# The projection phase of a gated attention mix: three weight tiles a chunk, measures between evictions, zero matmuls ahead, loads from two queues

## The chip, the core and the metric

The kernel runs on one core of one Trainium2 chip. The metric is the device time of one execution in microseconds. The core has five engines, each with a queue of its own that runs in order: TensorE (PE, matrix products into the eight banks of PSUM), VectorE (DVE), ScalarE (ACT), GpSimd (POOL) and SyncE (SP). SP, ACT and POOL also issue DMAs, which run on sixteen DMA engines. Semaphores order the engines among each other.

## The reference

Two attentions over the same input are mixed by a gate. A has 32 heads with their own keys and values; B has 32 query heads and one shared key and value head. Each head is 18 wide.

```python
x = A_x                                   # 1 x 2048 x 576
g = sigmoid((x * gate_w).sum(-1, keepdims=True))
q, k, v = heads(x @ A_wqkv)               # 32 heads of 18
a = (softmax(q k^T / sqrt(18)) v) @ A_wo
q = heads(x @ B_wq); k = x @ B_wk; v = x @ B_wv      # one k, one v for all heads
b = (softmax(q k^T / sqrt(18)) v) @ B_wo
return g * a + (1 - g) * b
```

## The kernel before

The kernel has two phases. The first projects x; the second, nearly nine tenths of the time, goes through 64 heads. Only the first phase is touched by the change; it is followed by the projection of A's values (`project_v`, L252), which already runs among the first row maxima of the heads, and by the loop over heads.

The transposed input `xT` is 576 x 2048. The left sides of all projections but A's values are laid out as one matrix `wall` of 14 weight tiles of 128 columns (`MT = 14`): B's key, the gate, B's value and B's queries in tiles 0 to 4, A's queries and keys, interleaved by heads, from the end of tile 4 on. The contraction of 576 is split in five blocks of 128 rows (`NKT = 5`); the fifth has 64 rows, which are loaded twice, into both halves of the 128 partitions.

For accuracy each operand is split in a rounded high part and the remainder: `xh`, `xl` of x (L275 on ACT, L276 and L277 on DVE), `wh`, `wl` of a weight tile (L133 on ACT, L134 on DVE). A projection of one weight tile for one chunk of 512 columns of x is 14 matmuls into one PSUM bank (`PROJ`, L210): high by high, low by high, high by low; the second copy of the fifth block holds x's remainder, so that high and low of it are done in one matmul. A bank is then evicted as two 16-bit halves, `ph` by ACT (L214) and `pl` by DVE (L220), scaled by `tv`, a power of two for each row, and the halves are written to DRAM (`qkh` from ACT's queue, `qkl` from POOL's). Tile 0 holds the gate and B's value too: it is copied out unscaled (`pst`, L217), and `shared_v` transposes B's value with four PE transposes (L239).

`tv` balances queries against keys. `measure` takes the largest magnitude of each weight column: DVE reduces over the five blocks (L162), PE transposes the result (L165), DVE reduces again (L166). `balance` reduces these over the columns of each kind (a mask made in DRAM tells which columns are which), has PE transpose and spread the two maxima (L176, L183), and computes the powers of two with some ten short DVE instructions (L185 to L195). It runs twice: for B over tiles 0 to 4, for A over all 14.

The order of the work is written out by hand; each engine runs its part in the order of the program. Loads: SP issues `ones_r`, weight tiles 0 to 4, six x tiles of 256 columns (six buffers `xs`), later x tiles 6 and 7 and weight tiles 5 to 13. A tile is three DMAs (`load5`): four blocks at once and the fifth twice. Then: split weight tile 0, measure tiles 0 to 4, balance, split x tiles 0 and 1 and weight tile 1; for each of four chunks split the next two x tiles, project tiles 0 and 1, and then transpose B's value. `project_rest` splits weight tile 2, measures tiles 5 to 13, balances a second time and projects tiles 2 to 13, splitting the next weight tile a tile ahead. POOL, which does no splits in this phase, issues the loads of B's key and of the first head's queries (`ksb`, `kdb`, `qs`) between chunk 3 and `project_rest`.

PSUM has three banks `ps` for projections and scores, four banks `pm` for transposes and maxima, and `acc`.

Of the kernel before, what the change touches and what calls it, by code (L numbers as in the profile page):

```python
# [21 lines left out]
H = 32  # L22
DH = 18
# [26 lines left out]
def gated_mix_kernel(ctx: ExitStack, tc: tile.TileContext, xT, wall, wv, wo, out):  # L50
# [3 lines left out]
    def dma(o, i, eng=None):  # L54
        o, i = (x.bitcast(F32) if x.dtype == F32R else x for x in (o, i))
        return (eng or nc.sync).dma_start(o, i)  # L56
# [67 lines left out]
        if l is not None:  # L124
            eng_l.tensor_tensor(l, src, h.bitcast(F32), op=OP.subtract)

    def load5(t, src):
        dma(t[:, 0:4, :], src[0:512, :].rearrange("(k p) m -> p k m", p=P))
        dma(t[0:64, 4, :], src[512:576, :])
        dma(t[64:128, 4, :], src[512:576, :])  # L130

    def split_w(st, w, eng_l):
        nc.scalar.activation(w["h"], st, AF.Copy)  # L133
        eng_l.tensor_tensor(w["l"], st, w["h"].bitcast(F32), op=OP.subtract)  # L134

    norm = wpool.tile([P, MT], F32, name="norm", bufs=1)
# [5 lines left out]
    nc.gpsimd.memset(zo[:, 0, :], 0.0)  # L142
    nc.gpsimd.memset(zo[:, 1, :], 1.0)
    nc.gpsimd.memset(tv, 0.0)
    mask_d = dram.tile([4, MT * P], F32, name="mask_d")
    dma(mask_d.rearrange("g (a b) -> (g a) b", b=56), zo[:, 0, :], nc.gpsimd)
    dma(mask_d[0:1, ROW_KB:ROW_KB + DH], zo[0:1, 1, 0:DH], nc.gpsimd)
# [3 lines left out]
            zo[0:H, 1, 0:DH], nc.gpsimd)  # L151
    dma(mask, mask_d.rearrange("g (m p) -> p g m", p=P), nc.gpsimd)

    def load_w(mt):
        st = wpool.tile([P, NKT, P], F32, name="wst", bufs=MT)
        load5(st, wall[mt])
        return st

    def measure(mt, st):

        a = wpool.tile([P, P], F32, name="wabs")
        nc.vector.tensor_reduce(a, st.rearrange("p k f -> p f k"), axis=AX.X, op=OP.max,  # L162
                                apply_absolute_value=True)
# [4 lines left out]
    def balance(g, n):  # L168

        m = wpool.tile([P, 2, MT], F32, name="bm", bufs=1)  # L170
        for i in range(2):
            nc.vector.tensor_tensor(m[:, i, 0:n], norm[:, 0:n], mask[:, g + i, 0:n], op=OP.mult)
        r = wpool.tile([P, 2], F32, name="br", bufs=1)
        nc.vector.tensor_reduce(r, m[:, :, 0:n], axis=AX.X, op=OP.max)
        pt = ps_m.tile([P, 512], F32, name="pm")
        nc.tensor.transpose(pt[0:2, 0:P], r, ident)  # L176
# [12 lines left out]
        nc.vector.tensor_scalar(e[:, 1:2], e[:, 0:1], 1.0, 64.0, op0=OP.mult, op1=OP.add)  # L189
        nc.vector.tensor_scalar(e[:, 0:1], e[:, 0:1], -1.0, 190.0, op0=OP.mult, op1=OP.add)  # L190
        t = wpool.tile([P, 2], F32, name="bt", bufs=1)
        nc.vector.tensor_single_scalar(t.bitcast(I32), e, 23, op=OP.logical_shift_left)
        nc.vector.tensor_scalar(t, t, LIFT, None, op0=OP.mult)
        for i in range(2):
            nc.vector.scalar_tensor_tensor(tv, mask[:, g + i, :], t[:, i:i + 1], tv, op0=OP.mult, op1=OP.add)  # L195

    def prep_w(st):
        w = {y: wpool.tile([P, NKT, P], F32R, name=f"w{y}") for y in "hl"}
        split_w(st, w, nc.vector)
# [5 lines left out]
    def project(mt, c, w):  # L205

        fp = ps_s.tile([P, 512], F32, name="ps")
        cs = slice(c * 512, (c + 1) * 512)
        for n, (a, b, k, kr) in enumerate(PROJ):
            nc.tensor.matmul(fp, w[a][:kr, k, :], X[b][:kr, k, cs], start=(n == 0), stop=(n == len(PROJ) - 1))  # L210
# [3 lines left out]
        nc.scalar.activation(h, fp, AF.Copy, scale=t)  # L214
        if mt == 0 or c == 0 and mt in HAS_K:
            st = stp.tile([P, 512], F32, name="pst", bufs=3)
            nc.scalar.activation(st, fp, AF.Copy)  # L217
            if c == 0:
                KD[mt] = st
        nc.vector.scalar_tensor_tensor(l, fp, t, h, op0=OP.mult, op1=OP.subtract)  # L220
        if c == 1 and mt in HAS_K:
            d = stp.tile([P, 512], F32, name="pd", bufs=1)
            nc.vector.tensor_tensor(d, fp, KD.pop(mt), op=OP.subtract)
            dh, dl = (stp.tile([P, 512], F16, name=f"pd{y}", bufs=1) for y in "hl")
            nc.scalar.activation(dh, d, AF.Copy, scale=t)
            nc.vector.scalar_tensor_tensor(dl, d, t, dh, op0=OP.mult, op1=OP.subtract)
        dma(qk_d[0][mt * P:(mt + 1) * P, cs], h, nc.scalar)
        dma(qk_d[1][mt * P:(mt + 1) * P, cs], l, nc.gpsimd)
        if c == 1 and mt in HAS_K:
            dma(kd_d[0][mt * P:(mt + 1) * P, :], dh, nc.scalar)  # L230
            dma(kd_d[1][mt * P:(mt + 1) * P, :], dl, nc.gpsimd)
        if mt == 0:
            dma(z_d[cs], st[ROW_G:ROW_G + 1, :], nc.scalar)
            return c, st
# [25 lines left out]
            pass  # L260

    WV = []
    with tc.tile_pool(name="xs", bufs=6, side="right") as xsp:
        W = [load_w(mt) for mt in range(5)]
        XS = []

        def load_x(c):
            XS.append(xsp.tile([P, NKT, 256], F32, name="xs"))
            load5(XS[c], xT[:, 256 * c:256 * c + 256])

        def split_x(c):
            xs = XS[c]
            cs = slice(c * 256, (c + 1) * 256)
            xh = X["h"][:, :, cs]
            nc.scalar.activation(xh, xs, AF.Copy)  # L275
# [3 lines left out]
        for c in range(6):  # L279
            load_x(c)  # L280
        WP = [prep_w(W[0])]
        for mt in range(5):
            measure(mt, W[mt])
        balance(0, 5)
        for c in range(2):
            split_x(c)
        WP.append(prep_w(W[1]))
        for c in range(6, 8):
            load_x(c)
        for mt in range(5, MT):  # L290
            W.append(load_w(mt))
# [15 lines left out]
    load_q(0, nc.gpsimd)  # L307

    def project_rest():
        WN = prep_w(W[2])  # L310
        for mt in range(5, MT):
            measure(mt, W[mt])
        balance(2, MT)
# [462 lines left out]
```

## Time and profile before

| | us |
|---|---|
| three runs | 2733.84, 2734.75, 2733.58 (median 2733.84) |
| the profiled execution | 2735.79 |
| its span, from the first instruction to the last | 2734.0 |
| PE busy in the span | 2663.3 |
| first projection matmul (L210) | 23.8 |
| last projection matmul of tiles 0 to 13 begins | 238.3 |
| value projection (L252) | 238.6 to 314.8 |

The profile is of one execution. Its page lists busy times by engine; groups of instructions are given by line, engine, operation and tiles, as `out<-in`, with the shapes, the count, the busy time and mean length in ns, and behind a bar the idle time of the engine just before them with what ended it. PE means matmuls, PEld the loading of weights into TensorE. `SPq` or `ACTq` is the sequencer of the queue that issues a DMA. The chain of waits is followed back from the last instruction, at each step to what released it. Tables by stretch give busy time and count of each engine in that stretch, then the granted TensorE clock, the mean busy share of the sixteen DMA engines and what they moved in GB/s.

### The profile page before, as it was taken

To read this page: it belongs to the slowest core of one execution; us is meant where nothing else is said; L and a number is where in the kernel's file an instruction comes from. 1 tells how busy PE (TensorE), PEld (TensorE's weight loads), DVE (VectorE), ACT (ScalarE), POOL (GpSimd) and SP (SyncE) were. 2 spreads that over 40 slices of the span, in tenths; PEclk is the share of its full clock that TensorE was granted. 3 is DMA by queue.
4 is the path that set the end of the run, shared out by engine and by line. 5 is a ranking of instruction groups with operands and counts; after the bars stand their busy time and mean duration, and the time that the engine had idled before them with its cause. 6 is when DMAs were issued, how large, how long until landed. Compare 5 with 4: busy or idle time off the path is not lost.

```text
span 2734.0 us, 57725 instructions
## 1 busy us (share of the span) xinstructions
PE 2663.3 (97%) x22160; PEld 958.8 (35%) x22160; DVE 2430.7 (89%) x4582; ACT 2384.1 (87%) x4768; POOL 231.0 (8%) x438
## 2 busy tenths in 40 slices
PE   5899999999999999999999999999999999999999
PEld 3688522222222222222222333333333332223444
DVE  5345899999999999999999999999999999998875
ACT  3232499999999999999999999999999999998875
POOL 2221000001000200110110001000100020001000
PEclk9899999999999999999999999999999999999998
DMA  7232100001100100110132112112221122122312
GB/s 197 76 118 90 51 20 20 20 18 53 35 17 23 54 27 20 45 43 20 30 66 85 40 51 84 54 40 57 72 66 47 44 61 64 39 64 88 89 36 94
DMA packets 135321, 151.49 MB, mean 55 GB/s; under 512 B 55709, under 2 KB 104765, under 8 KB 133846
## 3 DMA queue, kind: packets, MB, share of 16 engines
q1 hardware_dynamic: 116156, 123.59, 16.2%
q10 hardware_dynamic: 14120, 13.65, 1.5%
q0 software_dynamic: 4768, 10.56, 1.2%
q8 instruction: 174, 2.85, 0.5%
q14 instruction: 103, 0.84, 0.1%
HBM read 92.02 MB, written 46.45 MB: 51 GB/s over the span
## 4 chain that ended last, share of the span: by engine, by line
ACT 54%; PE 37%; DVE 6%; DMA 2%; SPq 1%; issue 1%; DVEq 0%; ACTq 0%
ACT pt L453 48%; PE acc L459 12%; PE ps L446 11%; ACT xb L412 6%; PE ps L210 6%; PE pm L575 4%; DVE mx L418 3%; PE ps L252 2%; PE pm L409 2%; SPq L56 1%; DVE oe L469 1%; DVE junk L415 1%; DMA xs<-xT 0%; DVE oacc L629 0%; DVE oacc L583 0%
## 5 line engine op out<-in xcount | busy, mean ns | idle before, releaser
L453 ACT ACTIVATE pt<-ps 128x512 f32<-128x512 f32 x4052 | 2093.1, 637 | 68.4 <-PE pm L409 60.2
L418 DVE TENSOR_REDUCE mx<-pm 128x1 f32<-128x512 f32 x3096 | 1940.2, 682 | 89.5 <-PE pm L409 74.6
L446 PE MATMUL ps<-qs,ksb 56*128 56x512 f16 x2688 | 818.4, 380 | 10.8
L409 PE MATMUL pm<-ksb,qs 54*128 54x512 f16 x2364 | 738.5, 383 | 2.6 <-DVE mx L418 1.6
L459 PE MATMUL acc<-pt,vb 128*19 128x512 f32 (+1 forms) x6136 | 592.3, 458 | 1.9
L459 PE MATMUL acc<-pt,vg 128*19 128x256 f32 (+1 forms) x5664 | 579.5, 481 | 2.3 <-DVE oe L469 0.5
L409 PEld LDWEIGHTS <-qs 54*128 54x128 f16 x4096 | 330.0, 93 | 248.1 <-issue 195.2
L446 PE MATMUL ps<-qs,ksa 56*128 56x512 f16 x1364 | 404.4, 379 | 4.8 <-ACT pt L453 1.3
L446 PEld LDWEIGHTS <-ksb 56*128 56x128 f16 x2688 | 175.0, 94 | 622.5 <-issue 573.9
L409 PE MATMUL pm<-ksa,qs 54*128 54x512 f16 x1232 | 384.8, 382 | 0.6 <-ACT xb L412 0.4
L415 DVE CUSTOM_DVE_ANT_0 junk<-pm,xb 128x512 bf16<-128x512 f32 x500 | 339.9, 680 | 0.0
L412 ACT ACTIVATE xb<-pm 128x512 f32<-128x512 f32 x500 | 316.5, 633 | 0.0
L446 PEld LDWEIGHTS <-ksa 56*128 56x128 f16 x1408 | 89.3, 94 | 328.9 <-issue 299.0
L459 PEld LDWEIGHTS acc<-pt,vb 128*19 128x19 f32 x6136 | 104.1, 96 | 223.7 <-issue 206.6
L459 PEld LDWEIGHTS acc<-pt,vg 128*19 128x19 f32 x5664 | 96.0, 97 | 222.9 <-issue 204.9
L428 POOL TENSOR_SCALAR mt<-mt 128x32 f32<-128x32 f32 x64 | 18.6, 290 | 1616.4 <-DVE mt L426 1616.4
L214 ACT ACTIVATE ph<-ps,tv 128x512 f16<-128x512 f32 x56 | 38.5, 687 | 122.0 <-PE ps L210 114.5
L409 PE MATMUL pm<-kdb,qs 54*128 54x512 f16 x372 | 141.5, 380 | 0.0
L220 DVE SCALAR_TENSOR_TENSOR pl<-ps,tv,ph 128x512 f16<-128x512 f32 x56 | 42.0, 751 | 93.8 <-ACT ph L214 75.4
L210 PE MATMUL ps<-xh,wh 128*128 128x512 f32 x280 | 76.4, 403 | 3.3 <-DVE xh L277 2.6
L210 PE MATMUL ps<-xh,wl 128*128 128x512 f32 x280 | 75.1, 399 | 0.0
L469 DVE COPY oe<-acc 128x512 f32<-128x512 f32 x63 | 43.6, 692 | 30.0 <-PE acc L459 29.4
(123 smaller groups left out, 1253.8 us busy)
## 6 DMA issues: line engine op xcount, KB each, us to landing
qs<-qkh SPq DMA_DIRECT2D x244, 72.0 KB
qs<-qkl SPq DMA_DIRECT2D x122, 72.0 KB
onh<-oh SPq DMA_DIRECT2D x32, 256.0 KB
onl<-ol SPq DMA_DIRECT2D x32, 256.0 KB
oih<-onh SPq DMA_DIRECT2D x16, 512.0 KB
oil<-onl SPq DMA_DIRECT2D x16, 512.0 KB
ot<-oe SPq DMA_DIRECT2D x220, 36.0 KB
R<-r_d SPq DMA_DIRECT2D x55, 144.0 KB
```

The source lines that it names most:

```text
L210: nc.tensor.matmul(fp, w[a][:kr, k, :], X[b][:kr, k, cs], start=(n == 0), stop=(n == len(PROJ) - 1))
L220: nc.vector.scalar_tensor_tensor(l, fp, t, h, op0=OP.mult, op1=OP.subtract)
L252: nc.tensor.matmul(fp[:, 0:288], X[b][:kr, k, st_ * P:(st_ + 1) * P], w[a][:kr, k, :], start=(n == 0), stop=(n == len(PROJ) - 1))
L409: nc.tensor.matmul(pm, qs[u % 3][b:b + 54, i * P:(i + 1) * P], k, start=True, stop=True)
L412: nc.scalar.activation(MX["x", u, i], pm, AF.Relu)
L415: nc.vector.tensor_tensor_reduce(junk, pm, MX.pop(("x", u, i)), 1.0, -3e38, op0=OP.add, op1=OP.max, accum_out=MX[u][:, i, c:c + 1])
L418: nc.vector.tensor_reduce(MX[u][:, i, c:c + 1], pm, axis=AX.X, op=OP.max)
L446: nc.tensor.matmul(ps, kst(u)[b:b + 56, i * P:(i + 1) * P], qs[u % 3][b:b + 56, c * 512:(c + 1) * 512], start=True, stop=True)
L453: nc.scalar.activation(pt, ps, AF.Exp, scale=SCALE / LIFT ** 2)
L459: nc.tensor.matmul(acc[32 * j:32 * j + 19, a:b], v_of(u, i), PT[u, i, j][:, a:b], start=(i == 0 and a == 0), stop=(i == 15), skip_group_ch ...
L469: nc.vector.tensor_copy(oe, acc)
L575: nc.tensor.matmul(fp[:, 0:288], o[b][:r, t, s2 * P:(s2 + 1) * P], w[a][:r, t, 288 * hf:288 * hf + 288], start=(n == 0), stop=(n == 3 * nt ...
```

## The change

- A fifth block is loaded by one DMA, from a source that repeats the 64 rows (`to_broadcast`), instead of two.
- x tile 0 is issued from ACT's queue; the order on SP is weight 0, weight 1, x 1, weight 2, x 2, weights 3 and 4, x 3, weights 5 and 6, x tiles 4 to 7, weights 7 to 13. x has four buffers instead of six.
- 17 matmuls of zeros into `acc` are issued ahead of the first projection.
- Tiles 0, 1 and 2 are projected in each chunk, instead of 0 and 1; chunk 0 is done in halves of 256 columns, for all three tiles, before its first eviction. `shared_v` comes directly after tile 0's projection.
- Tiles 0 to 4 are measured for B by one reduction to a scalar a partition (`measure_b`); tiles 4 to 13 for A by L162's reduction alone, kept for all columns (`measure_a`), between the evictions of tiles 1 and 2 in chunks 1 to 3 and of tile 3. `balance` reduces these directly; measuring has no PE transposes left. The second balance comes after tile 3.
- The low halves of all weight tiles but tile 0 are computed on POOL; the split weights have four buffers instead of two.
- Odd chunks go to `pm` banks.
- The 14 products of a bank come in another order: those that need only the high parts first, the fifth block last.

```diff
-PROJ = [("h", "h", k, 128) for k in range(NKT)] + [("h", "l", k, 128) for k in range(NKT - 1)] + \
-       [("l", "h", k, 128) for k in range(NKT)]
+PROJ = [("h", "h", k, 128) for k in range(NKT - 1)] + [("l", "h", k, 128) for k in range(NKT - 1)] + \
+       [("h", "l", k, 128) for k in range(NKT - 1)] + [("h", "h", NKT - 1, 128), ("l", "h", NKT - 1, 128)]
...
-    def load5(t, src):
-        dma(t[:, 0:4, :], src[0:512, :].rearrange("(k p) m -> p k m", p=P))
-        dma(t[0:64, 4, :], src[512:576, :])
-        dma(t[64:128, 4, :], src[512:576, :])
+    def load5(t, src, eng=None):
+        dma(t[:, 0:4, :], src[0:512, :].rearrange("(k p) m -> p k m", p=P), eng)
+        dma(t[:, 4, :], src[512:576, :].unsqueeze(0).to_broadcast([2, 64, src.shape[1]]), eng)
...
-    def measure(mt, st):
-        a = wpool.tile([P, P], F32, name="wabs")
-        nc.vector.tensor_reduce(a, st.rearrange("p k f -> p f k"), axis=AX.X, op=OP.max,
-                                apply_absolute_value=True)
-        pt = ps_m.tile([P, 512], F32, name="pm")
-        nc.tensor.transpose(pt[:, 0:P], a, ident)
-        nc.vector.tensor_reduce(norm[:, mt:mt + 1], pt[:, 0:P], axis=AX.X, op=OP.max)
+    def size(o, i):
+        nc.vector.tensor_reduce(o, i, axis=AX.XY, op=OP.max, apply_absolute_value=True)
+    def measure_b(mt, st):
+        if mt == 0:
+            size(norm_b[:, 0, 0:1], st[:, :, ROW_KB:ROW_KB + DH])
+        f0, f1 = max(ROW_Q - P * mt, 0), min(ROW_Q + DH * H - P * mt, P)
+        size(norm_b[:, 1, mt:mt + 1], st[:, :, f0:f1])
+    def measure_a(mt, st):
+        nc.vector.tensor_reduce(norm_a[:, P * (mt - 4):P * (mt - 3)], st.rearrange("p k f -> p f k"),
+                                axis=AX.X, op=OP.max, apply_absolute_value=True)
+    def balance(g):
         r = wpool.tile([P, 2], F32, name="br", bufs=1)
+        if g == 0:
+            nc.vector.tensor_reduce(r, norm_b, axis=AX.X, op=OP.max)
+        else:
+            r0 = q_row(H) - 4 * P
+            sizes = norm_a[:, r0:r0 + 2 * DH * H].rearrange("p (h a d) -> p a h d", a=2, d=DH)
+            for i in range(2):
+                nc.vector.tensor_reduce(r[:, i:i + 1], sizes[:, 1 - i], axis=AX.XY, op=OP.max)
...
+    def bank(odd=False):
+        return ps_m.tile([P, 512], F32, name="pm") if odd else ps_s.tile([P, 512], F32, name="ps")
+    def products(fp, w, s0, a0, b0):
+        for n, (a, b, k, kr) in enumerate(PROJ):
+            nc.tensor.matmul(fp[:, a0:b0], w[a][:kr, k, :], X[b][:kr, k, s0 + a0:s0 + b0],
+                             start=(n == 0), stop=(n == len(PROJ) - 1), skip_group_check=True)
...
+        W = [load_w(0)]
+        load_x(0, nc.scalar)
+        early = qs[2][:, 0:512]
+        nc.vector.memset(early, 0.0)
+        nc.scalar.activation(early[:, 0:32], ones, AF.Copy, scale=0.0)
+        for _ in range(17):
+            nc.tensor.matmul(acc, early[:, 0:P], early, start=True, stop=True)
...
+        WP = [prep_w(W[0], nc.vector)]
+        split_x(0)
+        for mt in (1, 2):
+            WP.append(prep_w(W[mt]))
+        split_x(1)
...
+        FP = [bank() for mt in range(3)]
+        for i in range(2):
+            for mt in range(3):
+                products(FP[mt], WP[mt], 0, 256 * i, 256 * i + 256)
         for mt in range(5):
-            measure(mt, W[mt])
-        balance(0, 5)
...
+            measure_b(mt, W[mt])
+        balance(0)
+        WP.append(prep_w(W[3]))
         for c in range(4):
             if c < 3:
                 split_x(2 * c + 2)
                 split_x(2 * c + 3)
-            keep = project(0, c, WP[0])
-            project(1, c, WP[1])
-            shared_v(*keep)
+            for mt in range(3):
+                keep = project(mt, c, WP[mt], FP[mt] if c == 0 else None)
+                if mt == 0:
+                    shared_v(*keep)
+                elif c:
+                    measure_a(2 + 2 * c + mt - 1, W[2 + 2 * c + mt - 1])
...
     def project_rest():
...
-        for mt in range(2, MT):
-            w = WN
+        for mt in range(3, MT):
+            w = WP[mt]
             if mt + 1 < MT:
-                WN = prep_w(W[mt + 1])
+                WP.append(prep_w(W[mt + 1]))
             for c in range(4):
                 project(mt, c, w)
+                if mt == 3:
+                    measure_a(10 + c, W[10 + c])
+            if mt == 3:
+                balance(2)
```

More of the change, by code (lines that the diff above doesn't have):

```diff
@@ L134, in split_w @@
         eng_l.tensor_tensor(w["l"], st, w["h"].bitcast(F32), op=OP.subtract)
-    norm = wpool.tile([P, MT], F32, name="norm", bufs=1)
+    norm_b = wpool.tile([P, 2, 5], F32, name="norm_b", bufs=1)
+    norm_a = wpool.tile([P, (MT - 4) * P], F32, name="norm_a", bufs=1)
     tv = wpool.tile([P, MT], F32, name="tv", bufs=1)
@@ L144, in gated_mix_kernel @@
     nc.gpsimd.memset(tv, 0.0)
+    nc.gpsimd.memset(norm_b, 0.0)
     mask_d = dram.tile([4, MT * P], F32, name="mask_d")
@@ L152, in gated_mix_kernel, with load_w @@
     dma(mask, mask_d.rearrange("g (m p) -> p g m", p=P), nc.gpsimd)
-    def load_w(mt):
+    def load_w(mt, eng=None):
         st = wpool.tile([P, NKT, P], F32, name="wst", bufs=MT)
-        load5(st, wall[mt])
+        load5(st, wall[mt], eng)
         return st
-    def measure(mt, st):
-        a = wpool.tile([P, P], F32, name="wabs")
-        nc.vector.tensor_reduce(a, st.rearrange("p k f -> p f k"), axis=AX.X, op=OP.max,
-                                apply_absolute_value=True)
-        pt = ps_m.tile([P, 512], F32, name="pm")
-        nc.tensor.transpose(pt[:, 0:P], a, ident)
-        nc.vector.tensor_reduce(norm[:, mt:mt + 1], pt[:, 0:P], axis=AX.X, op=OP.max)
[L168 to L172, printed above, removed]
-        r = wpool.tile([P, 2], F32, name="br", bufs=1)
-        nc.vector.tensor_reduce(r, m[:, :, 0:n], axis=AX.X, op=OP.max)
+    def size(o, i):
[9 more added lines that the diff above has]
+    def balance(g):
+        r = wpool.tile([P, 2], F32, name="br", bufs=1)
+        if g == 0:
[5 more added lines that the diff above has]
+                nc.vector.tensor_reduce(r[:, i:i + 1], sizes[:, 1 - i], axis=AX.XY, op=OP.max)
         pt = ps_m.tile([P, 512], F32, name="pm")
@@ L195, in balance, with prep_w @@
             nc.vector.scalar_tensor_tensor(tv, mask[:, g + i, :], t[:, i:i + 1], tv, op0=OP.mult, op1=OP.add)
-    def prep_w(st):
-        w = {y: wpool.tile([P, NKT, P], F32R, name=f"w{y}") for y in "hl"}
-        split_w(st, w, nc.vector)
+    def prep_w(st, eng=None):
+        w = {y: wpool.tile([P, NKT, P], F32R, name=f"w{y}", bufs=4) for y in "hl"}
+        split_w(st, w, eng or nc.gpsimd)
         return w
@@ L203, in gated_mix_kernel, with project @@
     KD = {}
-    def project(mt, c, w):
-        fp = ps_s.tile([P, 512], F32, name="ps")
+    def bank(odd=False):
[4 more added lines that the diff above has]
+                             start=(n == 0), stop=(n == len(PROJ) - 1), skip_group_check=True)
+    def project(mt, c, w, fp=None):
         cs = slice(c * 512, (c + 1) * 512)
-        for n, (a, b, k, kr) in enumerate(PROJ):
-            nc.tensor.matmul(fp, w[a][:kr, k, :], X[b][:kr, k, cs], start=(n == 0), stop=(n == len(PROJ) - 1))
+        if fp is None:
+            fp = bank(c % 2)
+            products(fp, w, 512 * c, 0, 512)
         h = stp.tile([P, 512], F16, name="ph")
@@ L262, in gated_mix_kernel, with load_x @@
     WV = []
-    with tc.tile_pool(name="xs", bufs=6, side="right") as xsp:
-        W = [load_w(mt) for mt in range(5)]
+    with tc.tile_pool(name="xs", bufs=4, side="right") as xsp:
         XS = []
-        def load_x(c):
+        def load_x(c, eng=None):
             XS.append(xsp.tile([P, NKT, 256], F32, name="xs"))
-            load5(XS[c], xT[:, 256 * c:256 * c + 256])
+            load5(XS[c], xT[:, 256 * c:256 * c + 256], eng)
         def split_x(c):
@@ L277, in split_x @@
             nc.vector.tensor_tensor(xh[64:128, 4], xs[64:128, 4], xh[64:128, 4].bitcast(F32), op=OP.subtract)
-        for c in range(6):
-            load_x(c)
-        WP = [prep_w(W[0])]
-        for mt in range(5):
-            measure(mt, W[mt])
-        balance(0, 5)
[L285 to L291, printed above, removed]
+        W = [load_w(0)]
[5 more added lines that the diff above has]
+            nc.tensor.matmul(acc, early[:, 0:P], early, start=True, stop=True)
+        W.append(load_w(1))
+        load_x(1)
+        W.append(load_w(2))
+        load_x(2)
+        W += [load_w(3), load_w(4)]
+        load_x(3)
+        W += [load_w(5), load_w(6)]
+        WP = [prep_w(W[0], nc.vector)]
[3 more added lines that the diff above has]
+        split_x(1)
+        for c in range(4, 8):
+            load_x(c)
+        for mt in range(7, MT):
+            W.append(load_w(mt))
+        FP = [bank() for mt in range(3)]
+        for i in range(2):
+            for mt in range(3):
+                products(FP[mt], WP[mt], 0, 256 * i, 256 * i + 256)
+        for mt in range(5):
+            measure_b(mt, W[mt])
+        balance(0)
+        WP.append(prep_w(W[3]))
         for c in range(4):
```

4 lines of the change are left out of this document (removed).

## The prediction

> **What bounds the kernel now.** I read the profile's page first, then the chain of waits, then the timeline of the first 95 us, which is the only part that the change touches.
>
> ```profile
> span 2734.0 us, 57725 instructions
> ...
> PE 2663.3 (97%) x22160; PEld 958.8 (35%) x22160; DVE 2430.7 (89%) x4582; ACT 2384.1 (87%) x4768; POOL 231.0 (8%) x438
> ```
>
> PE is busy nearly always, and what is not busy lies at the start. The chain of waits in the order of time says when the first phase ends:
>
> ```profile
> 82.02 156.70 PE ps L210 x672
> ...
> 238.72 3.73 PE ps L252 x28
> ```
>
> From 82 us the chain is PE alone: 672 projection matmuls (48 projections of 14, one per tile and 512-column chunk), then the projection of V. So what is won or lost before 238.72 us moves everything behind it by as much; the value projections and the main loop are the same program in the same order, and I take their length as fixed. The 28 matmuls of 288 columns in 3.73 us, 0.133 each, will price half-width matmuls.
>
> The timeline of the first 35 us (start, length, engine, line; in brackets the idle time before):
>
> ```profile
> 6.57 1.28 ACT L133 ACT_TABLE_LOAD   x1 [6.57 <-DMA wst<-wall]
> ...
> 20.08 1.27 ACT L275 ACTIVATE xh<-xs 128x1280 fp32r<-128x1280 f32 x1 [11.48 <-DMA xs<-xT]
> ...
> 23.83 2.07 PE L210 MATMUL ps<-xh,wh 128*128 128x512 f32 x4 [0.66 <-ACT xh L275]
> ...
> 33.19 0.69 ACT L214 ACTIVATE ph<-ps,tv 128x512 f16<-128x512 f32 x1 [5.01 <-PE ps L210]
> 33.77 0.59 ACT L217 ACTIVATE pst<-ps 128x512 f32<-128x512 f32 x1
> ```
>
> And of 35 to 95 us:
>
> ```profile
> 36.35 0.41 PE L239 MATMUL pm<-ident,pst 18*128 18x18 f32 x4
> ...
> 57.24 0.42 PE L239 MATMUL pm<-ident,pst 18*128 18x18 f32 x4
> ...
> 80.26 0.37 PE L176 MATMUL pm<-ident,br 128*2 128x128 f32 x1 [0.89 <-DVE br L174]
> ...
> 81.95 2.50 PE L210 MATMUL ps<-xh,wh 128*128 128x512 f32 x5
> ...
> 83.42 0.50 DVE L195 SCALAR_TENSOR_TENSOR tv<-mask,bt,tv 128x14 f32<-128x14 f32 x2
> ...
> 87.94 1.32 PE L210 MATMUL ps<-xh,wh 128*128 128x512 f32 x5
> ```
>
> The reader is to see two holes. PE gets its first real matmul at 23.8 us, because the first x tile lands at 20.1 behind five weight tiles. And from 57.7 to 81.95 it waits 24.3 us for the measuring of nine weight tiles. Behind the hole the first projection takes 5.99 us (81.95 to 87.94); the 47 after it take (238.72 - 87.94)/47 = 3.21 each. A cold start costs the difference, 2.77 us.
>
> **The change part by part.** The durations of the helpers, from the groups of lines of the first 170 us, and from POOL's own groups:
>
> ```profile
> L220 DVE SCALAR_TENSOR_TENSOR pl<-ps,tv,ph 128x512 f16<-128x512 f32 x34 | 25.5, 751 | 61.9 <-ACT ph L214 49.8 <-ACT pst L217 12.0
> L214 ACT ACTIVATE ph<-ps,tv 128x512 f16<-128x512 f32 x34 | 23.3, 687 | 89.1 <-PE ps L210 81.7 <-DMA wst<-wall 5.1 <-PE pm L239 2.1
> ...
> L162 DVE TENSOR_REDUCE wabs<-wst 128x128 f32<-128x640 f32 x14 | 17.1, 1223 | 0.0
> ```
>
> ```profile
> L56 POOL DMA_DIRECT2D qkl<-pl x56 | 30.5, 545 | 161.0 <-DVE pl L220 150.8 <-DVE vb L242 5.7 <-DVE pdl L226 4.1
> ...
> L125 POOL TENSOR_TENSOR wol<-wost,woh 128x576 fp32r<-128x576 f32 (+1 forms) x9 | 12.7, 1412 | 0.7
> ...
> L56 POOL DMA_DIRECT2D ksb<-qkh x4 | 2.0, 505 | 2.9 <-DMA qkl<-pl 2.9
> ```
>
> The DMA list has the landing of a qkl write:
>
> ```profile
> qkl<-pl POOLq DMA_DIRECT2D x56, 128.0 KB, 2.1
> ```
>
> Measuring between evictions: DVE has 0.75 + 1.22 = 1.97 us a projection against PE's 3.21, so it is hidden; the 24.3 us hole goes. What stays of it stands after tile 3, since PE's transpose in the second balance is queued ahead of tile 4: eviction 0.69 + 0.75, measure 1.22, two reductions of 576 elements (0.84 each at L220's rate, 1.10 at L162's; I take 0.84, plain rows being nearer), 1.69 from PE's transpose to the next matmul, 0.2 of hops: 6.3 us. POOL adds to it: it issues 17 loads ahead of tile 3's qkl writes, 17 x 0.505 = 8.5 us by the ksb row, and a weight split of 1412 x 640/576 = 1.57. With 1.65 us before and 0.55 + 0.55 + 2.1 of issue and landing around it, the buffer for tile 3's last pl comes 1.4 us late (4.3 with that row's wait of 2.9 for a landing). 7.7 in all, bounds 6.3 to 10.6.
>
> shared_v now stands directly behind tile 0's own projection: PE waits for ph and pst (33.19 to 34.36, the end of the L217 row) and transposes (0.41): 1.7 us with hops, in each of three chunks, where before tile 1's matmuls covered it.
>
> The splits on POOL cost PE nothing later: 4 x 0.545 + 1.57 of 12.8 us a tile. Half-width matmuls cost 0.115 (half of 3.21/14) to 0.133: chunk 0 is 9.7 to 11.2 us instead of 9.6. The 17 zero matmuls, at most 17 x 0.43 (5.99/14) = 7.3 us from about 4 us (an estimate: table load and memsets first), lie under the wait for data; without that cover they would delay the first matmul by 3 to 4 us. Every bank still takes 14 products, in another order.
>
> The loads are where I see the risk. Of each tile the fifth block was loaded by two DMAs of 64 rows; now by one whose source has an outer count of 2 (a repeat) over 64 rows. What an outer count does to a transfer is shown late in the trace, where eight loads of R, seven of 18 rows by 8 KB, are queued at once (SP's timeline, then a table by stretch with DMA share and GB/s last):
>
> ```profile
> 633.97 2.90 SPq L56 DMA_DIRECT2D R<-r_d  x8
> ```
>
> ```profile
> 12.00:20.00 8.00, 1.90 (x4) 0.73 (x4) 5.25 (x8) 0.00 (x0) 0.54 (x2) 1.00 0.98 147
> 20.00:32.00 12.00, 6.48 (x15) 4.54 (x16) 9.28 (x23) 5.71 (x5) 0.00 (x0) 1.00 1.08 291
> 60.00:61.00 1.00, 0.00 (x0) 0.00 (x0) 0.36 (x1) 1.00 (x2) 0.97 (x2) 0.72 1.13 329
> 637.00:643.00 6.00, 5.95 (x60) 1.86 (x57) 6.00 (x11) 6.00 (x13) 0.00 (x0) 1.00 0.60 137
> ```
>
> A backlog of 18-row transfers keeps 0.60 of the 16 engines busy over six microseconds, between nine and ten of them, and 9 divides 18, while loads of 128 and 64 rows fill all (1.08, 1.13). And a backlog does not raise the share: each transfer takes the same ones. So I read: the outer count is dealt out evenly, from the same engine on. An outer count of 2 then leaves two engines, the same two each time.
>
> [...] No run here shows an outer count of 2.
>
> The price: at 329/16 = 20.6 GB/s an engine (18.2 from the 291 row) the pair carries, for a weight tile, 262/16 + 65.5/2 = 49 KB or 2.39 us (2.70), for an x tile twice that, 4.77 (5.40). x tile 5 has six x and seven weight tiles up to it: 45.3 us (51.3). The first bytes' delay is 6.57 less the 1.1 us of one tile's data, 5.5; the mask load, which halved the rate in 12 to 20 us, takes 8 x (1 - 147/291) = 4.0 us. x tile 5 lands at 55 us (61). I take 55, as fourteen engines are idle meanwhile.
>
> ACT's split of x tile 5 is queued ahead of chunk 1's first eviction, and with it everything: 55 + 1.27 + 1.28 + 0.36 puts PE's next matmul at 57.9. Two more projections with a cold start, 6.42 + 2.77: 67.1. Chunks 2 and 3, each 3 x 3.21 + 1.7: 89.7 (x tile 7, 9.5 us behind x tile 5, is in time; so are weights 7 to 13, 16.7 us later still; x tile 6 has to wait on SP for DVE's split of x tile 2, behind the first balance, which weight tile 4 at 5.5 + 4.0 + 5 x 2.39 + 3 x 4.77 = 36 us lets end near 42, before the pair of engines is free). Tile 3, 12.8: 102.5. Balance, 7.7: 110.2. Forty projections and a cold start, 128.4 + 2.77: 241.4, against 238.72: 2.7 us later.
>
> One more term: loads and result writes hold each other up. ACT's L214 row shows 5.1 us of waiting for weight loads that it does not read, so its writes are queued behind landings. With loads 2.4 times as long that is between 0 (off the path) and 12.3 us; I take the row's own 5.1. Sum: +7.8 us. The profiled execution took 2735.79 us around its span of 2734.0, 1.95 over the median of the runs, 2733.84; on that, 2741.6.
>
> [...]
>
> **The rivals.** First, all sixteen engines carry the fifth block, and the change does what it means to. Up to the third weight tile 2.29 MB take 7.9 us at 291 GB/s, so it lands at 13.4 to 17.4; with its split on ACT and POOL and four half banks (7.4) chunk 0 ends at 23 to 27, say 24. Balance to tv 3.66 (80.26 to 83.92), eviction 1.2, transposes 0.4: chunk 1 at 29.3. Three chunks with shared_v and a cold start 36.8, tile 3 12.8, balance 7.7, the rest 131.2: 217.8, or 20.9 us sooner: 2713 us. For it speaks every hole removed above; against it the 18-row loads.
>
> Second, two engines, but faster alone and with no wait between loads and writes, and a clock that does not fall: 2.7 less two cold starts, about 2730, no difference to be told. For it: the rate of a lone pair stands in no row. Third, the change doesn't do what it says of DVE: measures and splits queue so that evictions come late. Against it, the 1.97 of 3.21; if each of ten projections lost the 1.22 it would cost 12 us on top of the first rival, 2725.
>
> **How the numbers follow.** Forecast 0.56, own range 2731 (second rival's terms) to 2755 (61 us for x tile 5, and 12.3). First rival 0.33, 2706 to 2722. Second 0.07, third 0.04. What this kernel's measurement can tell from no change is 0.2%, 5.5 us, so faster is under 2728.4 and slower over 2739.3. Faster: 0.33 + 0.04 + little of the second and the forecast, 0.39. Slower: 0.70 of the forecast and a little, 0.40. Same: 0.21. The range must span both signs: 2708 to 2753 leaves out a quarter of the first rival and a tenth of the forecast.
>
> **What would show it.** Right: the DMA share in the first 50 us near 2/16 to 4/16 between bursts where it was near 1, ACT's split of x tile 5 waiting for its load until 50 us or later, the last L210 matmul at 238 us or later. Wrong: a share near 1 until some 30 us, x tile 5 before 35 us, the first L252 near 218. Either way: no L165, one hole of 6 to 10 us after tile 3, three of about 1.7 us at L239's place. It would be wrong altogether if the stretch behind the first phase changed its length.

## The result, and the profile after

The changed kernel takes 2749.11 us (median of four runs, 2748.05 to 2751.4), against 2734.30 for four runs of the kernel before beside it: a ratio of 1.0054, 95% interval 1.0041 to 1.0067. It is slower by half a per cent, 7.5 us more than the 2741.6 forecast, inside the range. The profiled execution took 2748.05.

The page's head and line of engines, and the chain of waits in order of time:

```profile
span 2746.3 us, 57774 instructions
...
PE 2671.1 (97%) x22205; PEld 965.0 (35%) x22205; DVE 2416.8 (88%) x4555; ACT 2383.8 (87%) x4769; POOL 252.6 (9%) x452
```

```profile
79.42 8.09 PE ps L220 x28
87.51 3.28 PE pm L220 x14
...
92.45 6.74 PE pm L220 x28
...
118.76 5.54 PE ps L220 x14
124.30 3.27 PE pm L220 x14
...
251.70 3.72 PE ps L269 x28
```

The value projection begins at 251.70 instead of 238.72, 12.98 us later, and the span is 12.3 us longer: everything was lost before it. From that point to the end of the span there are 2494.6 us, before 2495.3; in all twelve experiments below it is 2494.4 to 2496.4. So the start of the value projection is the measure of each kernel, and the rest of this section asks what PE waits for ahead of it. PE's timeline, where it stood idle (in brackets for how long, and for whom):

```profile
12.61 0.73 PE L220 MATMUL ps<-xh,wh 128*128 128x256 f32 x4 [3.21 <-ACT xh L291]
...
20.54 1.22 PE L220 MATMUL ps<-xh,wl 128*128 128x256 f32 x4 [4.33 <-POOL wl L133]
...
39.47 0.61 PE L256 MATMUL pm<-ident,pst 18*128 18x18 f32 x4 [4.16 <-ACT pst L234]
...
54.63 0.61 PE L256 MATMUL pm<-ident,pst 18*128 18x18 f32 x4 [8.93 <-ACT pst L234]
...
78.81 0.61 PE L256 MATMUL pm<-ident,pst 18*128 18x18 f32 x4 [12.09 <-ACT pst L234]
...
92.03 0.42 PE L256 MATMUL pm<-ident,pst 18*128 18x18 f32 x4 [1.26 <-ACT pst L234]
...
117.01 0.37 PE L186 MATMUL pm<-ident,br 128*2 128x128 f32 x1 [4.76 <-DVE br L184]
```

The two old holes are gone: the first real matmul comes at 12.6 us, not 23.8, and the 24.3 us of measuring are now 6.4 (tile 3's last matmul ends at 112.25, tile 4's first starts at 118.69). In their place PE stands 8.93 and 12.09 us ahead of the transposes of chunks 1 and 2. ACT's timeline has the reason for each:

```profile
50.01 1.27 ACT L291 ACTIVATE xh<-xs 128x1280 fp32r<-128x1280 f32 x1 [6.66 <-DMA xs<-xT]
...
52.25 1.27 ACT L291 ACTIVATE xh<-xs 128x1280 fp32r<-128x1280 f32 x1 [0.96 <-DMA xs<-xT]
...
56.64 0.72 ACT L242 ACTIVATE pdh<-pd,tv 128x512 f16<-128x512 f32 x1 [2.06 <-DVE pd L240]
64.38 0.34 ACTq L56 DMA_DIRECT2D qkh<-ph  x1
65.30 0.33 ACTq L56 DMA_DIRECT2D kdh<-pdh  x1
67.85 0.24 ACTq L56 DMA_DIRECT2D z_d<-pst  x1
68.19 0.69 ACT L231 ACTIVATE ph<-pm,tv 128x512 f16<-128x512 f32 x1 [10.83 <-DMA wst<-wall]
73.73 0.34 ACTq L56 DMA_DIRECT2D qkh<-ph  x1
74.17 0.69 ACT L231 ACTIVATE ph<-pm,tv 128x512 f16<-128x512 f32 x1 [5.29 <-DMA wst<-wall]
...
75.27 2.43 ACT L291 ACTIVATE xh<-xs 128x1280 fp32r<-128x1280 f32 x2 [0.40 <-ACT ph L231]
```

The first hole is plain: ACT has to split x tiles 4 and 5 (50.01, 52.25) ahead of chunk 1's first eviction, and they land late. The second is not. Between 57.4 and 68.2 ACT computes nothing, though the data of its writes were ready by 57.4 and the bank of its next eviction by 60.2. The first write is issued only at 64.38, the next two at 65.30 and 67.85, and then comes the eviction. The landing that released the queue is that of a weight tile which none of these instructions reads. The records of the DMAs name the semaphores: those of SP and of ACT are counted on the same eight (100, 102, 103, 104, 106, 107, 109 and 110) in turn, and each of the three writes goes out when the load before it on its semaphore has landed. The write at 64.38 stands behind the weight load that SP issued at 55.47 and that landed at 64.30, the one at 65.30 behind that of 56.89 (landed at 65.22), the one at 67.85 behind that of 61.29 (67.83). So chunk 1's three evictions end at 74.9, x tiles 6 and 7 are split at 75.3, and chunk 2's first eviction, behind them, lets PE go on at 78.8.

How full the DMA engines were, in two stretches (length; busy time and count of PE, PEld, DVE, ACT, POOL; granted clock, DMA share, GB/s):

```profile
20.00:40.00 20.00, 11.11 (x73) 10.60 (x73) 10.79 (x24) 6.13 (x7) 3.58 (x3) 0.76 0.52 114
14.00:17.00 3.00, 2.21 (x10) 1.92 (x10) 0.28 (x1) 0.19 (x1) 1.51 (x1) 0.52 0.15 50
```

The same 20 us of the kernel before:

```profile
20.00:40.00 20.00, 14.48 (x49) 10.80 (x50) 12.56 (x28) 9.93 (x10) 1.11 (x2) 1.00 0.87 239
```

The share fell from 0.87 to 0.52. Between 14 and 17 us 0.15 of sixteen engines is 2.4 engines, at 50 GB/s. Between 34 and 36 us, where only the 1 KB packets of x tiles are on their way, it is 0.14 at 46 GB/s, and by the records of the packets two are in flight at a time for 1.66 of the 2 us and three for the rest. The two engines of the forecast would be 0.125 of sixteen, and both stretches agree.

### The profile page after: what moved, and what is told of

Read it like the earlier page. It is cut to its first block, busy times and chain, and to the rows that moved or that the text cites. A ratio compares the mean times of both kernels' runs of the same rounds, so it can differ in the third digit from the quotient of the medians.

```text
span 2746.3 us, 57774 instructions
## 1 busy us (share of the span) xinstructions
PE 2671.1 (97%) x22205; PEld 965.0 (35%) x22205; DVE 2416.8 (88%) x4555; ACT 2383.8 (87%) x4769; POOL 252.6 (9%) x452
## 4 chain that ended last, share of the span: by engine, by line
ACT 53%; PE 36%; DVE 6%; SPq 2%; DMA 1%; issue 1%; POOL 0%; ACTq 0%; DVEq 0%; POOLq 0%
ACT pt L490 47%; PE acc L496 12%; PE ps L483 10%; ACT xb L449 6%; PE pm L612 4%; DVE mx L455 4%; PE ps L220 3%; PE pm L220 3%; PE ps L269 2%; SPq L56 2%; PE pm L446 1%; DVE oe L506 1%; DMA xs<-xT 1%; DVE junk L452 1%; DVE oacc L666 0%
## 5 line engine op out<-in xcount | busy, mean ns | idle before, releaser
L490 ACT ACTIVATE pt<-ps 128x512 f32<-128x512 f32 x4052 | 2093.1, 637 | 68.2 <-PE pm L446 60.4
L231 ACT ACTIVATE ph<-pm,tv 128x512 f16<-128x512 f32 x28 | 19.3, 689 | 77.4 <-PE pm L220 58.7
L237 DVE SCALAR_TENSOR_TENSOR pl<-pm,tv,ph 128x512 f16<-128x512 f32 x28 | 21.0, 750 | 70.6 <-ACT ph L231 66.8
L272 ACT ACTIVATE vst<-ps 128x288 f32<-128x288 f32 x32 | 13.2, 412 | 62.2 <-PE ps L269 62.2
L237 DVE SCALAR_TENSOR_TENSOR pl<-ps,tv,ph 128x512 f16<-128x512 f32 x28 | 21.0, 751 | 41.2 <-ACT pst L234 21.6
```

Source lines behind the costliest of these rows:

```text
L490: nc.scalar.activation(pt, ps, AF.Exp, scale=SCALE / LIFT ** 2)
```

## The experiments

In what follows "value projection at" is the start of that step in the chain of waits of the experiment. My theory after this reading: the repeating source is all of the loss, partly through late x tiles, partly through writes held up by landings. The rival: measuring, the splits on POOL and the new place of `shared_v` cost as much as they bring.

**1. The fifth block as two loads of 64 rows again.** Of the change only this is undone.

```diff
-        dma(t[:, 4, :], src[512:576, :].unsqueeze(0).to_broadcast([2, 64, src.shape[1]]), eng)
+        dma(t[0:64, 4, :], src[512:576, :], eng)
+        dma(t[64:128, 4, :], src[512:576, :], eng)
```

> The changed kernel with the fifth block loaded by two DMAs of 64 rows again, all else as changed. Theory (the repeating source puts the block on two DMA engines): the share of busy DMA engines goes back to about 1 in the first 30 us, x tile 5 lands before 33 us instead of 52, the value projection starts near 219 us instead of 251.7, the time is 2716 us (2708 to 2724). Rival one (loads and result writes hold each other up whatever the engines, with the same eight semaphores in turn): ACT's waits for weight loads stay above 10 us and the time above 2735. Rival two (POOL's splits or the early measures are what is late): x tile 5 lands early, but the value projection starts after 235 us.

Measured: 2724.17 us (2720.77 to 2725.99), ratio to before 0.996 (0.9946 to 0.9975). The same stretch of its table, and its chain and PE timeline:

```profile
20.00:40.00 20.00, 14.71 (x84) 12.51 (x82) 12.66 (x29) 7.43 (x9) 2.59 (x4) 0.80 0.90 229
```

```profile
17.76 1.22 PE L221 MATMUL ps<-xh,wl 128*128 128x256 f32 x4 [6.22 <-POOL wl L134]
```

```profile
90.14 6.21 PE ps L221 x14
...
223.73 3.72 PE ps L270 x28
```

The share is 0.90 again, and the value projection begins 28.0 us sooner than with the repeating source: the repeating source turns a gain of 0.4% into a loss of 0.5%. The theory holds. SP, too, issues the loads faster again: one DMA of an x tile takes it 515 ns in the median, against 1515 in the changed kernel and 561 before. The kernel is 8 us slower than expected, though, just outside the range that I gave. By the profiled executions it is 4.7 us late at the value projection (219 expected); 6.2 us of waiting for POOL's split of weight tile 1 at 17.76 is new in view, and experiments 4 to 11 take up what is left.

**2. The other way round: the kernel before, with the repeating source alone.**

```diff
-        dma(t[0:64, 4, :], src[512:576, :])
-        dma(t[64:128, 4, :], src[512:576, :])
+        dma(t[:, 4, :], src[512:576, :].unsqueeze(0).to_broadcast([2, 64, src.shape[1]]))
```

> The kernel before with only this of the change: the fifth block by one DMA from a repeating source. Theory: by 2.39 us a weight tile and 4.77 an x tile on the pair, x tile 0 lands near 25 us instead of 20, weight tile 13 near 85 instead of 61, the second hole ends some 5 us later; the time is 2740 us (2737 to 2750). Rival (the repeat costs only in the new order of loads): 2734, within 2.

Measured: 2762.53 us, ratio 1.0103 (1.0088 to 1.0119); value projection at 266.18. That is 28 us more than before, five times the 5 that were expected. PE's hole and ACT's timeline of this kernel:

```profile
64.74 0.61 PE L238 MATMUL pm<-ident,pst 18*128 18x18 f32 x4 [17.50 <-ACT pst L216]
```

```profile
48.16 0.34 ACTq L56 DMA_DIRECT2D qkh<-ph  x1
52.44 0.47 ACTq L56 DMA_DIRECT2D z_d<-pst  x1
52.96 0.69 ACT L213 ACTIVATE ph<-ps,tv 128x512 f16<-128x512 f32 x1 [12.81 <-DMA xs<-xT]
60.74 0.35 ACTq L56 DMA_DIRECT2D qkh<-ph  x1
61.20 2.43 ACT L274 ACTIVATE xh<-xs 128x1280 fp32r<-128x1280 f32 x2 [7.55 <-DMA wst<-wall]
```

The expectation counted late tiles only. Here, too, writes whose data are ready (`pst` was done at 40.2, `z_d` goes out at 52.44) stand behind landings of loads, and the evictions behind the writes. That it is 28 us as in experiment 1 is partly chance: the holes are others, 17.50 us here and 3.14 a chunk later, where the changed kernel has 8.93 and 12.09.

**3. The changed kernel, with the writes of tiles 0 to 2 on another queue.** The loads stay as slow as they are; only the queue of `qkh`, `kdh` and `z_d` changes from ACT's to POOL's.

```diff
-        dma(qk_d[0][mt * P:(mt + 1) * P, cs], h, nc.scalar)
+        aq = nc.gpsimd if mt < 3 else nc.scalar
+        dma(qk_d[0][mt * P:(mt + 1) * P, cs], h, aq)
...
-            dma(kd_d[0][mt * P:(mt + 1) * P, :], dh, nc.scalar)
+            dma(kd_d[0][mt * P:(mt + 1) * P, :], dh, aq)
...
-            dma(z_d[cs], st[ROW_G:ROW_G + 1, :], nc.scalar)
+            dma(z_d[cs], st[ROW_G:ROW_G + 1, :], aq)
```

> The changed kernel, with the result writes of tiles 0 to 2 that ACT issues given to POOL's queue. Theory (ACT's writes are queued behind landings of weight tiles, and PE waits at chunk 2 for it): the wait of 12.1 us ahead of chunk 2's transposes falls under 4, ACT's 16 us of waiting for weight loads in chunk 1 go, the time falls by 8 us to 2741 (2738 to 2744). Rival (chunk 2 waits for x tiles 6 and 7 themselves): the wait stays above 9 us and the time within 2 of 2749.

Measured: 2737.28 us (10 runs, 2735.97 to 2737.88), ratio 1.0007 (0.9998 to 1.0016), 11.8 us less than the changed kernel, where 8 were expected. PE's timeline at the two holes:

```profile
55.18 0.61 PE L257 MATMUL pm<-ident,pst 18*128 18x18 f32 x4 [10.09 <-ACT pst L234]
...
69.24 0.42 PE L257 MATMUL pm<-ident,pst 18*128 18x18 f32 x4 [1.31 <-ACT pst L234]
```

```profile
240.41 3.72 PE ps L270 x28
```

The first hole, that of x tile 5, stays (10.09 for 8.93); the second falls from 12.09 to 1.31. So it takes the writes on ACT's queue to make it, and it costs 11.3 us at the value projection. That fits the waits named above: POOL's DMAs are counted on eight other semaphores (111 to 118 in the changed kernel). Of the 28.0 us of experiment 1 the other 16.7 (240.41 less 223.73) are left; the longest wait among them is the one for x tile 5.

**4. `shared_v` behind tile 1's projection,** on top of experiment 1.

```diff
                 if mt == 0:
-                    shared_v(*keep)
-                elif c:
+                    first = keep
+                elif mt == 1:
+                    shared_v(*first)
+                if mt and c:
                     measure_a(2 + 2 * c + mt - 1, W[2 + 2 * c + mt - 1])
```

> The kernel with two loads again, and the transposes of the shared value behind tile 1's projection, as before the change. Theory: three waits of 1.7 us go, 4 to 5 us under the kernel with two loads alone. Rival (PE is held there by DVE or by loads): less than 2 us.

Measured: 2715.47 us, ratio 0.9931 (0.9915 to 0.9948): 8.7 us less by the medians, 6.2 by the value projection of the profiled executions (217.58 for 223.73); 4 to 5 were expected. The waits of chunks 1 to 3 (1.26, 1.69, 1.26 us in experiment 1) are gone but for 0.2, and that is the gain that the edit explains. Most of the rest is in the projection behind the first transposes: between 35 and 37 us the granted clock is 1.00 here and 0.50 in experiment 1 (the four matmuls on `xl` take 1.09 us here, from 34.98, and 1.91 there, from 35.69). Nothing shows that the edit made it so.

**5. Why a projection takes 3.267 us.** In the changed kernel and in experiments 1 to 4, save the second, projections follow one another every 3.267 us (from 124.30 to 251.70 there are 39 of them), where before it was 3.21. Two runs on top of experiment 4, the order of products of before, and all chunks in banks `ps`:

```diff
-PROJ = [("h", "h", k, 128) for k in range(NKT - 1)] + [("l", "h", k, 128) for k in range(NKT - 1)] + \
-       [("h", "l", k, 128) for k in range(NKT - 1)] + [("h", "h", NKT - 1, 128), ("l", "h", NKT - 1, 128)]
+PROJ = [("h", "h", k, 128) for k in range(NKT)] + [("h", "l", k, 128) for k in range(NKT - 1)] + \
+       [("l", "h", k, 128) for k in range(NKT)]
```

```diff
-            fp = bank(c % 2)
+            fp = bank()
```

> The kernel with two 64-row loads and the late shared_v, but with the 14 products of a projection in the order of before (the fifth blocks inside their groups). Its projections follow one another every 3.267 us where those of before did every 3.21. If the order of the products makes the difference: 3.21 us a projection between 100 and 215 us, so 40 x 0.057 = 2.3 us less, about 2713 us. If it doesn't: 3.267 again and 2715.5, within 0.05%.

> The same kernel, but odd chunks take their bank from ps too, as before did, and not from pm in turn. If the turn of pools makes a projection 3.267 us long: 3.21 again, 2713 us. If it doesn't: the pace stays at 3.267, and with three banks instead of seven PE could wait for an eviction once or twice in the first phase: 2715 to 2719.

Measured: 2716.29 and 2718.89 us, and 3.267 us in both. Neither is the cause. With one kind of bank PE waits for a bank in chunk 1:

```profile
35.43 2.04 PE L221 MATMUL ps<-xh,wh 128*128 128x512 f32 x4 [2.49 <-DVE pl L238]
```

so the turn of banks, which had no step in the prediction, is worth 2.5 us by that wait and 3.4 by the medians (4.6 by the value projections, of which 1.4 was lost ahead of the first transposes).

**6. The second balance covered.** On top of experiment 4.

```diff
-                project(mt, c, w)
+                project(mt, c, w, ahead[c] if mt == 4 and c < 3 else None)
...
             if mt == 3:
+                ahead = [bank(c % 2) for c in range(3)]
+                for c in range(3):
+                    products(ahead[c], WP[4], 512 * c, 0, 512)
                 balance(2)
```

> The same kernel, but the products of tile 4's first three chunks are put ahead of the second balance, whose scales only their evictions need. Theory: the 6.0 us for which PE stands at the second balance, and the 2.3 us that it then loses at a low clock (5.57 us for the next projection where 3.27 is usual), are both wait, and three projections (9.8 us) cover them: 8.3 us less, 2707 us. Rival: tile 4's evictions then come late and bunched, banks come free late, and PE waits for them: 2711 to 2715.

Measured: 2708.66 us, ratio 0.9904 (0.9889 to 0.9919). The chain goes through the balance without a stop to speak of, and the next projection is not slowed:

```profile
85.70 3.26 PE ps L221 x14
88.97 0.12 PE pm L187
...
89.87 0.38 PE pm L194 x2
90.25 3.46 PE pm L221 x14
```

The gain is 6.8 us, 6.3 by the value projection (211.31); 8.3 were expected. Of the rest, 0.8 us is the wait that stays between the two parts of the balance (89.09 to 89.87), and 0.8 was lost at the start, where this execution's first transposes came at 31.99 for 31.16.

**7. Without the zero matmuls,** on top of experiment 4.

```diff
-        for _ in range(17):
-            nc.tensor.matmul(acc, early[:, 0:P], early, start=True, stop=True)
```

> The same kernel without the 17 zero matmuls. Theory: with xT tile 0 split at 8.7 us PE starts at about 8.8 at a low clock, its first three passes take longer, but it waits for POOL's second split at 17 us anyway, so little goes: 2715 to 2718. Rival: the low clock lasts past 17 us, and some 6 us of half rate are lost: 2719 to 2722.

Measured: 2715.84 against 2715.47 us, the value projection at 218.51 against 217.58. No difference to be told: as forecast, they lie under waits. But they also bring nothing here, since PE stands again for POOL's split at 17 us, with or without them.

**8. The place of the split weights.** On top of experiment 6, a tile of 128 bytes a partition, allocated behind the weights, moves them.

```diff
         WP = [prep_w(W[0], nc.vector)]
+        pad = wpool.tile([P, 32], F32, name="pad", bufs=1)
+        nc.gpsimd.memset(pad, 0.0)
```

> The kernel that covers the second balance, with a tile of 128 bytes a partition put behind the split weights, so that these lie 128 bytes lower: at 160 bytes modulo 512, as in the kernel before, where they lay at 288. Neither the order of the products nor the turn of the banks made a projection 3.267 us long. If the place of the weights does: 3.21 us, 40 x 0.057 = 2.3 us less, about 2706.4 us. If not: 3.267 and 2708.7 again, and the cause stays open.

Measured: 2706.4 us, and the pace in the chain:

```profile
94.28 3.20 PE ps L221 x14
...
209.65 3.73 PE ps L270 x28
```

3.204 us a projection, 228.9 ns a matmul for 233.3, with not one matmul changed. What made the changed kernel's projections longer is where its buffers came to lie; 40 of them make 2.5 us of it. Against experiment 6, on another chip (the kernel before takes 2735.49 there, 2735.05 on the first), the medians differ by 2.3, the value projections by 1.7 (209.65), since the first transposes came 1.4 us later.

**9. The splits of weight tiles 1 and 2 on VectorE,** on top of experiment 6.

```diff
         for mt in (1, 2):
-            WP.append(prep_w(W[mt]))
+            WP.append(prep_w(W[mt], nc.vector))
```

> The kernel that covers the second balance, with the low halves of weight tiles 1 and 2 split by VectorE in place of GpSimd. Theory: GpSimd begins them only at 15.9 us, behind its own memsets and its issue of mask writes, though the first was ready to be split at 9.4, and PE waits 5.3 us for it at 12.2 to 17.5; on VectorE, which is idle from 10.5 to 15.1, it is done at about 11.3: PE goes on at 12 and waits 1 or 2 us for weight tile 2 at 14, so 3 to 4 us less, 2704.7 to 2705.7. What the prediction said (the splits on GpSimd cost nothing): 2708.7 again, since xT tile 1 at 15 us is the next thing to wait for.

Measured: 2704.63 us, 4.0 less (on the chip of experiment 8); value projection at 206.13, 5.2 sooner. In experiment 6 the timelines of POOL, DVE and PE have this:

```profile
12.42 2.55 POOL L56 DMA_DIRECT2D mask<-mask_d  x1 [4.07 <-DMA mask_d<-zo]
...
14.97 0.95 POOL L265 MEMSET vst<- 128x304 f32 x3
15.06 3.44 DVE L293 TENSOR_TENSOR xl<-xs,xh 128x1024 fp32r<-128x1024 f32 x1 [4.59 <-DMA xs<-xT]
15.87 5.74 POOL L134 TENSOR_TENSOR wl<-wst,wh 128x640 fp32r<-128x640 f32 x3
...
17.47 1.23 PE L221 MATMUL ps<-xh,wl 128*128 128x256 f32 x4 [5.30 <-POOL wl L134]
```

And with the splits on DVE:

```profile
13.75 0.73 PE L221 MATMUL ps<-xh,wh 128*128 128x256 f32 x4 [0.71 <-ACT wh L133]
...
14.89 1.23 DVE L293 TENSOR_TENSOR xl<-xs,xh 128x1024 fp32r<-128x1024 f32 x1 [0.34 <-DMA xs<-xT]
```

POOL comes to the split 6.5 us after it could begin (9.4), since the load of the mask, queued ahead, waits for its writes. With the splits on DVE PE waits there for 0.71 us instead of 5.30.

**10 and 11. Both together, and a third place for the weights.** Experiment 9 with the pad of experiment 8, and with one of 288 bytes.

```diff
+        pad = wpool.tile([P, 72], F32, name="pad", bufs=1)
```

> The kernel with the splits of tiles 1 and 2 on VectorE and the split weights 128 bytes lower (160 modulo 512), both together. If they add: 2704.6 - 2.3 = 2702.3 us, with 3.204 us a projection.

> The same with a pad of 288 bytes, so that the split weights begin at 0 modulo 512. Two places are known: 288 with 3.267 us a projection and 160 with 3.204. If what decides is where a row of 512 bytes lies to a boundary of 512, the row that crosses none is as fast as 3.204 or faster: 2702.3 us or less. If it is something else about the place (128 or 256 bytes, say), the pace is 3.204 or 3.267: 2702.3 or 2704.6 us.

Measured: 2702.11 us, ratio 0.988 (0.9866 to 0.9895), and 2703.93 us. The chains:

```profile
102.24 3.21 PE ps L221 x14
...
204.79 3.74 PE ps L270 x28
```

```profile
102.53 3.27 PE ps L221 x14
...
207.06 3.69 PE ps L270 x28
```

By the medians the two gains add within 0.2 us (2702.3 was expected), but on a third chip, where the kernel before is 2.1 us faster than on the second; by the value projections the pad brings 1.3 us here (204.79 for 206.13) and 1.7 in experiment 8. At 0 modulo 512 the pace is 3.267 as at 288, so it isn't the crossing of a 512-byte boundary; 160 is the fast place of the three. The pads also move the tiles below the weights, and which distance decides (and to what) stays open. The version with 128 bytes beats both kernels: 31.3 us or 1.2% under the kernel before on the same chip (2733.38), and some 47 us under the changed one.

## Why the prediction was right, and where it was off

The direction and its cause were right: the fifth block on two DMA engines, x tile 5 late, and evictions behind it. The rival with sixteen engines gave 217.8 us for the value projection and 2713 us; with two loads (experiment 1) it is 223.73 and 2724.17, so it described that kernel, 6 us too well by the projection and 11 by the time. That the time lay inside the range confirms little: 45 us span both signs and the first rival's time, and slower was put at 0.40 against 0.39 for faster.

| step | forecast | measured |
|---|---|---|
| x tile 5 split, and with it landed | 55 | 52.25 |
| PE goes on after chunk 1's transposes | 57.9 | 55.2 |
| chunk 1 ends | 67.1 | 63.3 |
| chunk 2 takes | 11.3 | 24.2 (to 87.51) |
| chunk 3 takes | 11.3 | 11.7 (to 99.19) |
| tile 3 takes | 12.8 | 13.1 (to 112.25) |
| second balance | 7.7 | 6.4 |
| forty projections and a cold start | 131.2 | 133.0 |
| value projection, without the term for loads and writes | 241.4 | 251.70 |

**The step that failed in size** is "loads and result writes hold each other up", taken as the 5.1 us that the row of before showed, with bounds of 0 and 12.3. It is chunk 2's line: 12.9 us over the forecast, the 12.09 of waiting where 1.3 is usual and a restart at a low clock (0.56 granted between 78 and 83 us; two projections in 8.09 us instead of 6.53). With that term out of the kernel (experiment 3) the value projection begins at 240.41, and the forecast without it was 241.4. The time is then 2737.28 us, no difference to be told from before (ratio 1.0007), so the sign of the result hangs on the very term that I sized too small. I took the row of before as it stood although loads were to last 2.4 times as long, which is the upper bound's own argument. Writes that wait for landings of loads waited the longer, the longer the loads took (ACT's evictions stood 18.7 us behind weight loads in the changed kernel, 5.1 before), so the term should have been scaled: at 12.3 the forecast would have been 2748.8, and experiment 3 measured 11.3.

The other lines come to 2.6 us under the forecast, so the value projection is 5.2 us late against 246.5, the forecast with the term. Of the 7.5 us by the medians 3.0 are chance: the profiled execution lay 1.95 us above the median before and 1.06 below it after. The loads were 2.7 us faster than priced. The cold start after the balance cost 2.3 us (5.54 less 3.27), not 2.77; between the runs it was 1.8 (5.06 in experiment 7) to 3.0 (6.23 in the first run of experiment 5). It is half of the time for which the clock stays at 0.50 under the matmuls: 4.6 us in the changed kernel (118.69 to 123.32), 3.5 in experiment 7 (85.98 to 89.52). One figure does not hold the runs. The balance was priced 1.3 us too high. Of POOL's lateness, for which I added 1.4, some 0.6 us shows: `ph` is done at 112.97, and the last `pl` starts at 113.61, behind the landing of an earlier write of `pl`.

```profile
113.61 0.75 DVE L237 SCALAR_TENSOR_TENSOR pl<-pm,tv,ph 128x512 f16<-128x512 f32 x1 [1.90 <-DMA qkl<-pl]
```

**What was set at nothing or had no step.** The turn of banks gains 2.5 to 3.4 us (experiment 5). The splits on POOL cost 4.0 (experiment 9): I counted POOL's time late in the phase, when it is idle, and not at 9 to 17 us, where its queue has mask writes ahead. In the changed kernel that wait is 4.33 us (at 20.54), and no run tells how much of it the late loads would have cost anyway. And the pace of 3.267, 2.3 us over forty projections, had no step at all.

What was forecast of the zero matmuls (hidden), of measuring between evictions (hidden: only the balance's own 6.4 remains) and of the unchanged remainder held.

## What to carry to other kernels

A source with a repeat as its outermost count saves an issue, and here it cost most of the DMA engines (a share of 0.15 between 14 and 17 us, where two loads of 64 rows have 1.11): undone alone it was worth 25 us. When loads get slower, price every queue whose DMAs are counted on the same semaphores, not only the readers of the loads, and scale a coupling seen before by the loads' new length. A small part of a change can hide the worth of the rest: taken apart, the other parts gain, and with the waits that are left taken out (a balance with nothing behind it, an operation queued behind another's wait) the kernel is 1.2% faster than before.

## What the runs showed of the hardware that was not expected

The pace of matmuls that read the same kind of tiles in the same order depends on where their operands lie: 228.9 ns with the split weights at 160 bytes modulo 512, 233.3 at 0 and at 288, through forty projections and more: four kernels at 160 (before, and experiments 2, 8 and 10), ten at the other two places. The addresses are those that the programs allocate; x's split tiles lie at the same place in all of them, so of the operands only the weights moved. What about the place decides stays open.

Beside POOL's splits of weight tiles one split on DVE was stretched: that of x tile 1 takes 3.44 us in experiment 6, and 1.23 in experiment 9, where POOL was not splitting then. The two durations agree that they contend; for what, no trace shows. DVE's split began first, at 15.06, and was stretched, while POOL's first, from 15.87, was done by 17.47, when PE goes on with its output: 1.60 us at most, against the 1.58 of one alone in experiment 9.
